# Spectral filter stage: groups 2 to 13 by pairs, with a second step of 64 x 64 matmuls, and the weights' bounds summed in PSUM

## The chip, the core and the metric

The kernel runs on one core of a Trainium2 chip. The core's engines each work through an instruction queue of their own: TensorE (PE, matmuls; its weight loads are shown as PEld), VectorE (DVE), ScalarE (ACT), GpSimd (POOL) and SyncE (SP), which here issues the DMA transfers. PE writes its sums to PSUM; the others read them there and write to SBUF, the on-chip memory from which PE reads. The metric is the device time of one execution in microseconds (us); lower is better. One execution of the kernel before was also recorded by the hardware profiler, and the profile's lines come from it.

## What is computed

Four residual layers over x of shape (2048, 640): a spectral filter A and a token-mixing MLP B, each applied twice, A, B, A, B. Cut to what matters:

```python
def A(x):                       # x already normalised over its last axis
    X = rfft2(x)                # 2048 x 321 complex
    return irfft2(X * (w_r + 1j * w_i))

def B(h):                       # h: normalised x
    u = gelu(einsum("sd,sf->df", h, w1) + b1)      # f = 1728
    return (einsum("df,fs->ds", u, w2) + b2).T

x = x + A(layernorm(x)); x = x + B(layernorm(x))
x = x + A(layernorm(x)); x = x + B(layernorm(x))
```

## The kernel before

Everything large is done by PE in float16, with each operand split into a high part and a low part (names ending in h and l); `mm3` (line 256) issues the three products high-high, high-low and low-high. The 2048 rows are split as 128 x 16, so a transform over them is two steps: one over 128 (S1), one over 16 (second step), with a factor between. The stages of one half of the kernel are:

1. **S1.** `run` (first layer) or the second part of `b1st` with `a0_tail` (second layer) normalises rows, folds them by symmetry (`a0_fold1`, `a0_fold2`) and multiplies by the tables tM. ACT writes the high part (`a0_s1h`) and DVE the low part (`a0_s1l`) of S1 to the tiles s1h and s1l.
2. **The filter, `a1` (lines 408 to 672).** It runs over 16 groups of 128 rows of the spectrum. For one group g, in order: `dstage` (D, the transform over the 640 columns by the table tD, 16 matmuls; its last columns come from stacked rests stk, loaded by DMA); `psplit` (ph on ACT, pl on DVE); `s2stage` (S, the second step of the transform by the table tS2: 12 matmuls of 128 x 128 with 321 columns); `product` (ta and tb on DVE, their difference and sum on POOL: the complex product with w); `xsplit` (xh on ACT, xl on DVE, with the scale sx) and `twice` (copies of 63 columns on ACT and POOL); `is2stage` (I, the inverse of the second step by tI2: 36 matmuls of 64 input rows, two halves q); `yevict` and `y2evict` on ACT and `y2split` on POOL, which write Y and the two parts of Y2. In the loop over g (line 584) PE runs D of g+1, I of g-3, S of g. The first group's S has a table of its own; the last group's S, product and split are done by thirds (`s2mm`, `last_product`).
3. **The way back, `a2`.** `id_mm` and `is1_mm` return to rows, the residual is added and the next normalisation is done.
4. **The MLP.** `b1st` (first layer): 14 products with w1 and 16 with w2. `b2nd` (last layer) does it in blocks. The weights come by `wload`, are scaled and split by `wsplit` (wh on ACT, wl on DVE). The scale of each weight tile is a power of two from a bound: `scan1` sums its squares on ACT, `total` adds over columns (DVE) and rows (one matmul with ones), `pow2` turns it into the scale on DVE. `scale_x` does the same for the filter's w, `scale_b` for b1, and the first `b1st` does one `scale1` for each weight tile. The last layer uses the scales again.

**Order.** Inside `a1`, `a2` and some other stretches `self.pin` is true: each engine then runs its instructions in the order in which the code issues them. Elsewhere the compiler may move them. [...]

**PSUM.** `big` (line 89) gives buffers of two banks, four of them in turn: a fifth request waits until the readers of the first are done. Buffers of the other tiles (`self.t` with a count) work in the same way: w has three, ta three, tb two, yt two.

Of the kernel before, what the change touches and what calls it, by code (L numbers as in the profile page):

```python
# [33 lines left out]
YS = 2.0 ** -14  # L34
I32 = mybir.dt.int32
# [21 lines left out]
class Layers:  # L57
    def __init__(self, nc, tc, A):
        self.nc, self.tc, self.A = nc, tc, A
        self.open = {}  # L60
# [38 lines left out]
    def setup(self):  # L99
        nc, A = self.nc, self.A  # L100
        base = self.base = self.push("base", side="left")
        self.psum = self.push("ps", bufs=4, space=PSUM)
# [81 lines left out]
    def scan(self, raw, out):  # L184

        n = raw.shape[1]
        self.T.activation(self.junk[:, :n], raw, AF.Square, accum_out=out)

    def scan1(self, m, cs=(0, 1)):
        if m < NFT + NJ:  # L190
            if 0 in cs:
                self.ssq = self.t(self.base, [128, 1, 2], F32, "sq", 2)
            for c in cs:
                self.scan(self.wraws[m][c], self.ssq[:, 0, c:c + 1])

    def scale1(self, m, at=None):
# [4 lines left out]
        for ps in self.total(self.ssq, at):  # L201
# [13 lines left out]
    def scale_x(self, pool):  # L215

        V, mm = self.V, self.PE.matmul
        ps = self.big()
        mm(ps[:NG, 0, :128], self.xq, self.eye, start=True, stop=True)
        m = pool.tile([NG, 1], F32, name="xm")  # L220
        V.tensor_reduce(m, ps[:NG, 0, :128], op=ALU.max, axis=mybir.AxisListType.X)
# [3 lines left out]
        mm(ps[:, 1, :NG], b, self.eye[:NG, :NG], start=True, stop=True)  # L225
        yield
        q = pool.tile([128, NG], F32, name="xqq")
        V.tensor_scalar(q, ps[:, 1, :NG], SMALL, XS ** -2, op0=ALU.max, op1=ALU.mult)
# [5 lines left out]
    def scale_b(self):  # L234

        b = self.base
        sq = b.tile([128, 1, 1], F32, name="sqs")
        bsq = b.tile([128, NFT], F32, name="bsq")
        self.T.activation(bsq, self.b1, AF.Square, accum_out=sq[:, 0])
        yield  # L240
        for ps in self.total(sq):
# [1412 lines left out]
```

## Time and profile before

| | us |
|---|---|
| median of 3 runs (1040.97 to 1043.22) | 1041.69 |
| profiled execution, its own time | 1044.98 |
| its span, first to last instruction | 1043.2 |
| S1 of the first layer | 0 to 57 |
| filter, first layer | 57 to 137 |
| way back, first layer | 137 to 197 |
| `b1st` and S1 of the second layer | 197 to 573 |
| filter, second layer | 573 to 647 |
| way back, second layer | 647 to 700 |
| `b2nd` | 700 to 1043 |

A line of the page or of a grouped view names an operation by engine, operation, what it writes and what it reads (buffer numbers left out), shape (partitions x elements) and type; behind x stands how often it ran, then its total busy time and the mean in ns of one, then how long its engine had been idle before it and what ended that. A timeline line begins with its start and its duration in us. Nearly all operations are recorded under line 49, a helper, so they are told apart by the names of their tiles: ps is a PSUM buffer, tD belongs to D, tS to S, tI to I.

### The profile page before, as it was taken

How to read it: one execution, taken by the hardware profiler on the slowest of the kernel's cores; microseconds unless marked ns; L12 is line 12 of the kernel's file. 1: busy time of each engine (PE TensorE's matmuls, PEld its weight loads, DVE VectorE, ACT ScalarE, POOL GpSimd, SP SyncE). 2: the span in 40 equal slices, each digit the busy share in tenths (PEclk: the TensorE clock that was granted, in tenths of full speed). 3: DMA queues.
4: the chain of work that ended last, by engine and by line, in shares of the span. 5: the costliest groups of instructions: out<-in, count | busy, mean ns of one | idle time of the engine just before them, and what ended most of it. 6: DMA issues, size and time to landing. Idle time of an engine off the chain costs nothing.

```text
span 1043.2 us, 20923 instructions
## 1 busy us (share of the span) xinstructions
PE 998.0 (96%) x8315; PEld 733.2 (70%) x8315; DVE 710.4 (68%) x1437; ACT 585.3 (56%) x910; POOL 273.3 (26%) x482
## 2 busy tenths in 40 slices
PE   4889989999999999999997998999999999999998
PEld 3768766677777777777775786666777777777776
DVE  7978947854333956666675796677655564987885
ACT  5857669765555555555542475894644454634532
POOL 6928867300000002221112586770000000000000
PEclk9999989999999999999998998999999999999999
DMA  7864336532222264444424543455422232445511
GB/s 225 312 198 133 100 114 193 197 105 81 82 81 77 71 221 142 139 134 122 122 79 148 158 129 99 150 179 184 132 87 84 72 107 88 139 145 176 165 44 51
DMA packets 55305, 137.38 MB, mean 132 GB/s; under 512 B 6540, under 2 KB 12328, under 8 KB 55208
## 3 DMA queue, kind: packets, MB, share of 16 engines
q1 hardware_dynamic: 55208, 136.06, 41.2%
q8 instruction: 65, 1.06, 0.4%
q14 instruction: 32, 0.26, 0.1%
HBM read 112.96 MB, written 23.07 MB: 130 GB/s over the span
## 4 chain that ended last, share of the span: by engine, by line
PE 66%; DVE 16%; ACT 6%; POOL 5%; DMA 4%; issue 3%; SPq 1%; POOLq 0%; ACTq 0%; DVEq 0%
PE ps L49 66%; DVE wl L49 3%; DVE f L49 3%; POOL eo L49 2%; DMA xt<-x 2%; DVE st L49 2%; DVE s1l L49 2%; ACT wh L49 1%; ACT z L49 1%; DVE hl L49 1%; ACT junk L49 1%; ACT xt L49 1%; DVE xt L49 1%; DMA raw<-w 1%; DVE ta L49 1%
## 5 line engine op out<-in xcount | busy, mean ns | idle before, releaser
L49 PEld LDWEIGHTS <-wh 128*128 128x128 f16 x2992 | 290.1, 98 | 113.9 <-issue 2.0
L49 PEld LDWEIGHTS <-wl 128*128 128x128 f16 x1616 | 157.9, 98 | 61.9 <-DVE wl L49 0.5
L49 PE MATMUL ps<-hh,wh 128*128 128x320 f16 x896 | 186.3, 299 | 0.8 <-ACT hh L49 0.8
L49 PE MATMUL ps<-hl,wh 128*128 128x320 f16 x896 | 184.7, 299 | 0.0
L49 PE MATMUL ps<-hh,wl 128*128 128x320 f16 x832 | 171.5, 299 | 0.2 <-DVE wl L49 0.2
L49 DVE SCALAR_TENSOR_TENSOR wl<-raw,s,wh 128x1024 f16<-128x1024 f32 (+2 forms) x88 | 103.6, 1181 | 87.6 <-ACT wh L49 86.7
L49 PE MATMUL ps<-uh,wl 128*128 128x320 f16 x448 | 133.1, 299 | 0.0
L49 PE MATMUL ps<-ul,wh 128*128 128x320 f16 x448 | 133.1, 299 | 0.0
L49 ACT ACTIVATE wh<-raw,s 128x1024 f16<-128x1024 f32 (+2 forms) x92 | 94.8, 1048 | 68.0 <-PE ps L49 62.1
L49 PE MATMUL ps<-uh,wh 128*128 128x320 f16 x416 | 124.3, 299 | 0.0
L49 ACT ACTIVATE junk<-raw 128x896 bf16<-128x896 f32 (+1 forms) x60 | 59.6, 994 | 47.8 <-DMA raw<-w 47.8
L49 POOL TENSOR_TENSOR r<-v,mh 128x1 f32<-128x1 f32 x64 | 35.7, 559 | 141.3 <-DVE nm L49 129.0
L49 DVE TENSOR_TENSOR xt<-xt,ps 128x320 f32<-128x320 f32 (+1 forms) x96 | 44.9, 490 | 39.9 <-ACT ec L49 25.8
L49 PE MATMUL ps<-u,wo 128*128 128x320 f16 x504 | 69.9, 299 | 0.0
L49 DVE TENSOR_TENSOR f<-eo 128x256 f32<-128x256 f32 (+1 forms) x128 | 40.0, 365 | 41.9 <-POOL eo L49 41.3
L49 PEld LDWEIGHTS <-wo 128*128 128x128 f16 x504 | 49.3, 98 | 19.1
L49 ACT ACTIVATE z<-xt,nb,r 128x640 f32<-128x640 f32 x31 | 28.5, 919 | 55.8 <-POOL z L49 43.7
L49 DVE BATCH_NORM_STATS2 st<-xt 128x6 f32<-128x320 f32 x128 | 56.2, 481 | 5.0 <-DMA xt<-x 4.8
L49 PE MATMUL ps<-ph,tS 128*128 128x321 f16 (+2 forms) x288 | 59.1, 290 | 0.0
L49 POOL TENSOR_TENSOR eo<-z 128x320 f32<-128x320 f32 x63 | 54.2, 880 | 17.0 <-ACT z L49 15.1
L49 PE MATMUL ps<-tM,f 128*128 128x128 f32 x160 | 39.1, 420 | 19.4 <-DVE f L49 19.4
L49 PE MATMUL ps<-tDi,yh 128*128 128x322 f16 x256 | 55.9, 309 | 1.6 <-ACT yh L49 1.6
(166 smaller groups left out, 1907.5 us busy)
## 6 DMA issues: line engine op xcount, KB each, us to landing
raw<-w SPq DMA_DIRECT2D x56, 512.0 KB
xt<-x SPq DMA_DIRECT2D x80, 320.0 KB
w<-w SPq DMA_DIRECT2D x48, 321.0 KB
x<-xt SPq DMA_DIRECT2D x48, 320.0 KB
raw<-w SPq DMA_DIRECT2D x32, 448.0 KB
raw<-w2z SPq DMA_DIRECT2D x32, 448.0 KB
out<-xt SPq DMA_DIRECT2D x15, 320.0 KB
stk<-rest SPq DMA_DIRECT2D x42, 64.0 KB
```

The source lines that it names most:

```text
L49: i = f(*a, **k)
```

## The change

- **Pairs.** Groups 2 to 13 are taken by pairs (a, b). S1 is stored so that the 64 rows which belong to two of a group's four row sets stand together. The table of the second step then consists of two blocks of 64 x 64 with zeros beside them, and only the blocks are multiplied: `s2pair` issues 48 matmuls of 64 x 64 with 321 columns, four (e, r) for each part and factor. Those with r = 0 write one PSUM buffer, those with r = 1 another; each buffer then holds one half of either group, so the filter's w, the rows of Y and the scale sx are put in that order too (`PG`, `lanes`, `k_rows`, gsel). Groups 0, 1, 14 and 15 keep 128 x 128 matmuls.
- **Order.** One iteration of the loop now issues D of a, I, D of b, I, and one S for both. The buffers of PSUM are three of the tag big and one of the tag one: in the filter every request names its tag, and only the second buffer of `s2pair` takes the single one; elsewhere every fourth request takes it.
- **Work moved between engines.** The scale sx moves from `xsplit` to the products (`times`), so xh is a copy and xl a subtraction; for even groups half of that subtraction is on POOL. The high part of Y2 is written by ACT from PSUM and no longer by POOL. w has four buffers, each loaded again right behind its product.
- **Bounds.** The sums of squares are written as bf16, one for each half of a tile. `total` has no reduction on DVE and adds the halves by one matmul each in PSUM, in spare columns of a buffer that is in use anyway. In `b1st` the bounds follow the end of a product instead of standing within the next.
- **Weights of the MLP.** The four quarters of wl of the first tile move from `a1` to `a2`, those of wh within `a1`; scan and wh of the second tile come some iterations later in `a2`.

The diff, cut to its core; the loop that it removes is in the code above.

```diff
+PG = 2, 14
...
-    def big(self):
+    def big(self, one=None):
+        if one is None:
+            self.turn += 1
+            one = self.turn % 4 == 0
+        tag, bufs = ("one", 1) if one else ("big", 3)
         self.n += 1
-        return self.psum.tile([128, 2, 512], F32, tag="big", name=f"ps{self.n}")
+        return self.psum.tile([128, 2, 512], F32, tag=tag, name=f"ps{self.n}", bufs=bufs)
...
     def total(self, sq, at=None):
 
+        ps = at() if at else self.big()[:, 0, :1]
         n = sq.shape[1]
-        b = self.t(self.base, [128, n], BF16, f"sqb{n}", 2 if n == 1 else 1)
-        with self.nc.allow_low_precision("a bound, with room to spare"):
-            self.V.tensor_reduce(b, sq, op=ALU.add, axis=mybir.AxisListType.X)
-        yield
-        ps = at() if at else self.big()[:, 0, :n]
-        self.PE.matmul(ps, self.ones, b, start=True, stop=True)
+        for i in range(n):
+            self.PE.matmul(ps, self.ones, sq[:, i:i + 1], start=i == 0, stop=i == n - 1)
         yield ps
...
-        self.s1h = p.tile([128, 80, 16, 8], F16, name=f"s1h{self.n}")
-        self.s1l = p.tile([128, 80, 16, 8], F16, name=f"s1l{self.n}")
+        self.s1h = p.tile([128, 80, 2, 16, 4], F16, name=f"s1h{self.n}")
+        self.s1l = p.tile([128, 80, 2, 16, 4], F16, name=f"s1l{self.n}")
...
-    def a0_s1h(self, j, pv, zs=ZS):
-        self.T.activation(self.s1h[:, :, j], pv, AF.Copy, scale=S1S / (zs * TS))
-    def a0_s1l(self, j, pv, zs=ZS):
-        self.V.scalar_tensor_tensor(
-            self.s1l[:, :, j], pv, S1S / (zs * TS), self.s1h[:, :, j], op0=ALU.mult, op1=ALU.subtract
-        )
+    def a0_s1h(self, j, pv, sc=S1S / (ZS * TS), q=slice(0, 80)):
+        pv = pv.rearrange("p a (b c) -> p a b c", c=4)
+        self.T.activation(self.s1h[:, q, :, j], pv, AF.Copy, scale=sc)
+    def a0_s1l(self, j, pv, sc=S1S / (ZS * TS), q=slice(0, 80)):
+        pv = pv.rearrange("p a (b c) -> p a b c", c=4)
+        h, l = self.s1h[:, q, :, j], self.s1l[:, q, :, j]
+        if sc == 1.0:
+            self.V.tensor_tensor(l, pv, h, op=ALU.subtract)
+            return
+        for b in range(2):
+            self.V.scalar_tensor_tensor(
+                l[:, :, b], pv[:, :, b], sc, h[:, :, b], op0=ALU.mult, op1=ALU.subtract
+            )
...
-        yv = self.Y.rearrange("p a b j (g q c) -> p g q (a b j) c", q=2, c=4)
-        y2 = [y.rearrange("p b j (g q c) -> p g q (b j) c", q=2, c=4) for y in self.Y2]
+        def lanes(y, g):
+            if PG[0] <= g < PG[1]:
+                y = y.rearrange("p b j (u e q c) -> p u q e (b j) c", e=2, q=2, c=4)
+                return y[:, g // 2, g % 2]
+            return y.rearrange("p b j (g q c) -> p g q (b j) c", q=2, c=4)[:, g]
...
         def y2evict(g, ps):
+            y2hi(g, ps)
...
             return yt
 
         def y2split(g, yt):
-            G.tensor_copy(y2[0][:, g], yt)
-            G.tensor_tensor(y2[1][:, g], yt, y2[0][:, g], op=ALU.subtract)
+            G.tensor_tensor(lanes(self.Y2[1], g), yt, lanes(self.Y2[0], g), op=ALU.subtract)
...
+            w = self.t(p, [128, 2, NL], F32, "w", 4)
...
+            ps = self.big(False)
...
+        sc = PQS / (S1S * TS)
+        def phi(ps):
             ph = self.t(p, [128, 2, 322], F16, "ph", 2)
             pl = self.t(p, [128, 2, 322], F16, "pl", 2)
...
             T.activation(ph[:, :, :NL], ps[:, :, :NL], AF.Copy, scale=sc)
...
+            return ps, ph, pl
+        def plo(ps, ph, pl):
             V.scalar_tensor_tensor(pl[:, :, :NL], ps[:, :, :NL], sc, ph[:, :, :NL], op0=ALU.mult, op1=ALU.subtract)
...
+            return ph, pl
+        def xhi(g, c, x):
+            T.activation(xs[g % 3][0][:, :, c], x, AF.Copy)
+        def xlo(g, c, x, r=slice(0, 2), e=V):
+            xh, xl = (q[:, r, c] for q in xs[g % 3])
+            e.tensor_tensor(xl, x[:, r], xh, op=ALU.subtract)
 
         def xsplit(g, c, x):
...
+            xhi(g, c, x)
+            xlo(g, c, x)
 
         def twice(g):
 
...
+        def s2pair(x):
+            ps = self.big(False), self.big(True)
+            for a, b in ((0, 0), (1, 0), (0, 1)):
+                for ri in range(2):
+                    for q in range(2):
+                        for e in range(2):
+                            for r in range(2):
+                                m = slice(64 * r, 64 * r + 64)
+                                mm(
+                                    ps[r][64 * e:64 * e + 64, ri, :NL], self.tS2[m, a, 0, 2 * ri + q, m],
+                                    x[e][b][m, q, :NL], start=a == b == q == 0, stop=b == q == 1,
+                                )
+            return ps
         def s2stage(g, ph, pl):
             sp = 1 if g == 0 else 0
-            ps = self.big()
+            ps = self.big(False)
             for ri in range(2):
                 for q in range(2):
                     a = tuple(self.tS2[:, h, sp, 2 * ri + q] for h in range(2))
-                    b = (ph[:, q, :NL], pl[:, q, :NL])
+                    b = tuple(x[q][:, :NL] if g == 0 else x[:, q, :NL] for x in (ph, pl))
                     self.mm3(ps[:, ri, :NL], a, b, q == 0, q == 1)
...
+        def times(o, ps, g, w, c=slice(0, NL)):
+            n = c.stop - c.start
+            V.scalar_tensor_tensor(
+                o, ps[:, :, c], self.sx[:, g:g + 1], w[:, c].unsqueeze(1).to_broadcast([128, 2, n]),
+                op0=ALU.mult, op1=ALU.mult,
+            )
+        def product(g, ps):
             ta, tb = (self.t(p, [128, 2, NL], F32, a, n) for a, n in (("ta", 3), ("tb", 2)))
...
+            times(ta, ps, g, w[g][:, 0])
+            times(tb, ps, g, w[g][:, 1])
             G.tensor_tensor(ta[:, 0], ta[:, 0], tb[:, 1], op=ALU.subtract)
...
+            gi = G.tensor_tensor(ta[:, 1], tb[:, 0], ta[:, 1], op=ALU.add)
+            if g + 4 < NG:
+                w[g + 4] = wload(g + 4)
+            return ta, gi
...
+        w = {g: wload(g) for g in range(4)}
+        ps2, pv, yt, ta = {}, {}, {}, {}
+        whole = slice(0, NL)
+        def phalves(ps):
+            x = tuple([self.t(p, [128, 322], F16, f"{a}{q}", 1) for q in range(2)] for a in ("ph", "pl"))
+            for q in range(2):
+                a, b, c = ps[:, q, :NL], x[0][q][:, :NL], x[1][q][:, :NL]
+                T.activation(b, a, AF.Copy, scale=sc)
+                V.scalar_tensor_tensor(c, a, sc, b, op0=ALU.mult, op1=ALU.subtract)
+            return x
+        def xbegin(g):
+            xh, _ = xs[g % 3]
+            xhi(g, whole, ta[g])
+            T.activation(xh[:, :, NL:], xh[:, :, 257:320], AF.Copy)
+        def xfinish(g):
+            x, (_, xl) = ta.pop(g), xs[g % 3]
+            if g % 2:
+                xlo(g, whole, x)
+            else:
+                xlo(g, whole, x, slice(1, 2), G)
+                xlo(g, whole, x, slice(0, 1))
+            G.tensor_copy(xl[:, :, NL:], xl[:, :, 257:320])
+        def evict(g):
+            yevict(g, pv[g])
+            yt[g] = y2evict(g, pv.pop(g))
+        d = dstage(0)
+        pa = phalves(d)
+        pb = phi(dstage(1))
+        ps2[0] = s2stage(0, *pa)
+        stack(4)
+        if first:
+            for _ in self.scale_x(p, d):
+                pass
+        pb = plo(*pb)
+        last = NG // 2 - 1
+        at = lambda c: lambda: old[:, 1, c:c + 1]
+        for i in range(1, NG // 2):
+            a, b, k = 2 * i, 2 * i + 1, 2 * i - 4
+            pa = phi(dstage(a))
+            if i == 1:
+                ta[0], _ = product(0, ps2.pop(0))
+                ps2[1] = s2stage(1, *pb)
+                pa = plo(*pa)
+                xbegin(0)
+                pb = phi(dstage(b))
+                ta[1], gi = product(1, ps2.pop(1))
+                pb = plo(*pb)
+            else:
+                pv[k] = old = is2stage(k)
+                evict(k)
+                x = product(a - 2, ps2.pop(a - 2))
+                if first and i in (3, 4):
+                    small = sb if i == 3 else self.scale1(0, at(401))
+                xfinish(k + 1)
+                ta[a - 2], _ = x
+                y2split(k, yt.pop(k))
+                d = dstage(b)
+                pb = phi(d)
+                for q in {5: (0,), 6: (1, 2), 7: (3,)}.get(i, ()):
+                    self.wsplit(0, self.quarter(q)[0], lo=False, part=self.quarter(q)[1])
+                pa = plo(*pa)
+                xbegin(a - 2)
+                if first and i in (3, 4):
+                    next(small)
+                pv[k + 1] = is2stage(k + 1)
+                ta[a - 1], gi = product(a - 1, ps2.pop(a - 1))
+                if first and i in (3, 4):
+                    next(small)
+                pb = plo(*pb)
+            stack(2 * i + 4)
+            if i < last:
+                ps2[a], ps2[b] = s2pair((pa, pb))
+            else:
+                ps2[a] = s2stage(a, *pa)
+            if i == 2:
+                nc.sync.dma_start(self.tDi, A["tDi"])
+            if i in (3, 4):
+                c = slice((i - 3) * 8, (i - 3) * 8 + 8)
+                nc.sync.dma_start(self.tIM[:, c], A["tIM"][:, c])
+            xfinish(a - 2)
             if k >= 0:
...
+                evict(k + 1)
+                y2split(k + 1, yt.pop(k + 1))
+            if i < last:
+                xbegin(a - 1)
+            if i == 1:
                 self.wload(0)
                 self.wopen(0)
...
+            if first and i in (2, 3):
+                if i == 2:
+                    sb = self.scale_b(at(400))
+                    next(sb)
+                self.scan1(0, (i - 2,))
 
...
+            if 3 < i < 8:
+                self.wsplit(0, self.quarter(i - 4)[0], hi=False, part=self.quarter(i - 4)[1])
             if first:
-                if i in (6, 7):
-                    self.scan1(1, (i - 6,))
-                if i == 8:
+                if i in (9, 10):
+                    self.scan1(1, (i - 9,))
+                if i == 11:
                     sc = self.scale1(1, at=lambda: ps1[:, 1, 400:401])
-                    next(sc)
-                if i == 10:
+                if i == 13:
                     next(sc)
             if i == 3:
                 self.wopen(1)
-            if i in (12, 13):
-                self.wsplit(1, (i - 12,), lo=False)
+            if i in (14, 15):
+                self.wsplit(1, (i - 14,), lo=False)
...
+        def scales(ps, *ms):
+            for q, m in enumerate(ms):
+                if m < NFT + NJ:
+                    for _ in self.scale1(m, lambda: ps[:, 1, 400 + q:401 + q]):
+                        pass
...
                     if ft == NFT - 1 and 6 <= j:
                         usplit(j - 6, uf[j - 6])
+            scales(ps, *{0: (2,), 1: (3,), 2: (4, 5)}.get(ft, (ft + 3,)))
...
+            scales(ps, m + 3)
...
-            r_in = j16 * 8 + c8
+            r_in = c8 // 4 * 64 + j16 * 4 + c8 % 4
...
+    a = slice(*PG)
+    out[a] = out[a].reshape(-1, 2, 2, 64).transpose(0, 2, 1, 3).reshape(-1, 128).copy()
...
-    t["tM32"] = (m1 * TS).astype(np.float32)
+    t["tM32"] = (m1 * S1S).astype(np.float32)
```

More of the change, by code (lines that the diff above doesn't have):

```diff
@@ L186, in scan @@
         n = raw.shape[1]
-        self.T.activation(self.junk[:, :n], raw, AF.Square, accum_out=out)
+        junk = self.junk[:, :n] if len(raw.shape) == 3 else self.junk[:, 0, :n]
+        with self.nc.allow_low_precision("a bound, with room to spare"):
+            self.T.activation(junk, raw, AF.Square, accum_out=out)
     def scan1(self, m, cs=(0, 1)):
@@ L396, in a0_tail @@
             q = slice(t0 * 16, t1 * 16)
-            T.activation(self.s1h[:, q, j], pv, AF.Copy, scale=sc)
-            V.scalar_tensor_tensor(
-                self.s1l[:, q, j], pv, sc, self.s1h[:, q, j], op0=ALU.mult, op1=ALU.subtract
-            )
+            self.a0_s1h(j, pv, q=q)
+            self.a0_s1l(j, pv, q=q)
     def s1_all(self, j, fh, fl):
@@ L438, in y2hi @@
         def y2hi(g, ps):
-            T.activation(y2[0][:, g], pairs(ps, 256, 384), AF.Copy, scale=YS)
+            T.activation(lanes(self.Y2[0], g), pairs(ps, 256, 384), AF.Copy, scale=YS)
         def y2lo(g, ps):
@@ L481, in dstage @@
         def dstage(g):
-            ps = self.big()
-            part = lambda t: tuple(s[:, t * 16 + g].rearrange("p a b -> p (a b)") for s in (self.s1h, self.s1l))
+            ps = self.big(False)
+            part = lambda t: tuple(s[:, t * 16 + g].rearrange("p q a b -> p (q a b)") for s in (self.s1h, self.s1l))
             for c, bk, o0, o1, k in CL:
@@ L749, in a2 @@
                 ps1 = is1_mm(eo.pop(i - 1), i - 1)
-            if first and i == 10:
+            if first and i == 13:
                 next(sc)
```

177 lines of the change are left out of this document (43 added, 134 removed).

## The prediction

> **What bounds the kernel now.** I read the page's span and engines first: PE is busy 96% of it. Then, by windows, the filter stage, which runs twice, and the matrix stage behind the first of them (391 to 553).
>
> ```profile
> span 1043.2 us, 20923 instructions
> PE 998.0 (96%) x8315; PEld 733.2 (70%) x8315; DVE 710.4 (68%) x1437; ACT 585.3 (56%) x910; POOL 273.3 (26%) x482
> 391.00:553.00 162.00, 162.00 (x1319) 119.79 (x1318) 102.60 (x288) 86.55 (x126) 36.17 (x84) 1.00 0.40 124
> 80.00:88.00 8.00, 8.00 (x130) 6.58 (x128) 7.04 (x10) 6.22 (x14) 6.66 (x10) 1.00 0.52 151
> 112.00:120.00 8.00, 8.00 (x127) 6.27 (x125) 8.00 (x11) 5.59 (x11) 7.34 (x11) 1.00 0.50 146
> ```
>
> A windows row gives the stretch, then busy time of PE, PEld, DVE, ACT, POOL, the granted clock, DMA share and GB/s. PE is never idle in 80 to 88, but DVE has 7.0 and POOL 6.7 of 8 us: matmuls that go save time only until the next queue is full. In 112 to 120 DVE is full as well. The timeline shows what a group costs there:
>
> ```profile
> 81.12 0.31 PE L49 MATMUL ps<-ph,tS 128*128 128x321 f16 x1
> 82.64 0.30 PE L49 MATMUL ps<-ph,tS 128*128 128x321 f16 x1
> 82.78 0.30 PE L49 MATMUL ps<-tD,s1h 128*128 128x160 f16 x2
> 83.85 0.23 PE L49 MATMUL ps<-tD,stk 96*128 96x161 f16 x1
> 84.02 0.28 PE L49 MATMUL ps<-tI,xh 64*128 64x128 f16 x4
> 84.98 0.22 PE L49 MATMUL ps<-tI,xl 64*128 64x128 f16 x2
> 85.13 0.31 PE L49 MATMUL ps<-ph,tS 128*128 128x321 f16 x1
> 82.98 0.83 DVE L49 TENSOR_TENSOR ta<-ps,w 128x642 f32<-128x642 f32 x1 [0.16 <-PE ps L49]
> 83.72 0.82 DVE L49 TENSOR_TENSOR tb<-ps,w 128x642 f32<-128x642 f32 x1
> 84.86 0.83 DVE L49 SCALAR_TENSOR_TENSOR pl<-ps,ph 128x642 f16<-128x642 f32 x1 [0.32 <-ACT ph L49]
> 85.61 1.16 DVE L49 SCALAR_TENSOR_TENSOR xl<-ta,sx,xh 128x642 f16<-128x642 f32 x1
> ```
>
> The second step S (12 matmuls) runs 81.12 to 82.78, 1.66 us, (82.64 - 81.12)/11 = 0.138 each. The column transform D (16) runs to 84.02, 1.24 us, of which about 0.10 is empty at the end: its last matmul starts at 83.85, and 160 columns take (83.85 - 82.78)/15 = 0.071. The inverse I (36 of 64 rows) takes 1.11 us, again with about 0.1 empty at its end. Together 4.01 us a group. I's matmuls come every (84.98 - 84.02)/34 = 0.028 us although each streams 128 columns, which at D's rate would be 0.057: two row halves of the array work at once.
>
> **The pairs on PE.** For groups 2 to 13, 2 x 12 full matmuls become 48 of 64 x 64: twelve quartets, in each the four quarters of the array. If a quartet takes one 0.138 slot, S for two groups takes 1.66 instead of 3.32. PE needs per pair 2 x 1.24 + 2 x 1.11 + 1.66 + 0.1 (one more change of the array's shape, now between S and D) = 6.46 us, against 8.02. The other bound, from rows: only what I shows, two at a time, gives 24 x 0.138 = 3.32; nothing at all overlapped, 6.6, and I's 0.028 speaks against that. I take 1.66: I's 36 pairs of load and matmul show neither an issue limit (0.028 x 4 = 0.11 a quartet) nor a cost of loading.
>
> [...]
>
> **The pairs on the other queues.** What waits is DVE: its order in an iteration is ta and tb of group a-2, xl of a-3, pl of a, ta and tb of a-1, pl of b, half of xl of a-2. PE's S writes two buffers, of which the second comes from the new one-buffer tag. It is still held by group a-1 until that group's tb. So each S waits for six DVE operations, the first of which waits for the last S. Behind S on PE stand D and I of the next pair, and all of DVE's next products wait for it: a delay here is paid in full. Durations:
>
> ```profile
> L49 DVE SCALAR_TENSOR_TENSOR xt<-ps,c,xt 128x640 f32<-128x640 f32 x16 | 14.1, 882 | 5.0 <-ACT xt L49 5.0
> L49 DVE TENSOR_TENSOR hl<-hf,hh 128x640 f16<-128x640 f32 x32 | 23.8, 817 | 0.0
> 122.57 0.88 DVE L49 SCALAR_TENSOR_TENSOR xl<-ta,sx,xh 128x642 f16<-128x642 f32 x1
> L49 ACT ACTIVATE ph<-ps 128x642 f16<-128x642 f32 x30 | 21.2, 707 | 42.1 <-PE ps L49 42.1
> L49 ACT ACTIVATE hh<-hf 128x640 f16<-128x640 f32 x32 | 22.6, 730 | 0.5
> L49 ACT ACTIVATE xh<-xh 128x126 f16<-128x126 f16 x32 | 9.9, 308 | 1.0
> L49 ACT ACTIVATE Y<-ps 128x512 f32<-128x512 f32 x30 | 17.4, 581 | 3.1 <-PE ps L49 3.1
> L49 ACT ACTIVATE Y2h<-ps 128x256 f16<-128x256 f32 x4 | 1.5, 380 | 1.3 <-PE ps L49 1.3
> L49 ACT ACTIVATE yt<-ps 128x256 f32<-128x256 f32 x28 | 10.5, 375 | 1.1 <-POOL Y2l L49 1.1
> L49 POOL TENSOR_TENSOR ta<-tb,ta 128x321 f32<-128x321 f32 x30 | 28.1, 936 | 0.0
> L49 POOL TENSOR_TENSOR ta<-ta,tb 128x321 f32<-128x321 f32 x30 | 23.7, 791 | 46.8 <-DVE tb L49 46.8
> L49 POOL TENSOR_TENSOR Y2l<-yt,Y2h 128x256 f16<-128x256 f32 x28 | 20.9, 746 | 2.2
> L49 POOL COPY xl<-xl 128x126 f16<-128x126 f16 x32 | 9.7, 303 | 1.5 <-DVE xl L49 1.5
> ```
>
> Consecutive DVE operations overlap by 0.08 (tb starts 0.74 after ta). The products carry the scale now, so they are priced as the 0.882 row: 0.80 each. The low part of x becomes a plain subtraction: 0.82 alone as hl, but xl took 1.16 at 85.61, beside POOL, and 0.88 at 122.57, so with that factor 1.3 it is 1.08. pl is 0.75. Chain: 2 x 0.80 + 1.08 + 0.75 + 2 x 0.80 = 5.03; from the end of S to ta 0.20 (82.78 to 82.98), back to PE 0.05, S 1.66: **6.94, taken as a period of 7.0 us**. PE then idles about half a microsecond a pair.
>
> The rest fits under 7.0. ACT per pair: 2 x (0.71 + 0.73 + 0.31 + 0.58 + 0.38 + 0.38) = 6.2 (the high part of Y2 is new there). POOL: 2 x (0.94 + 0.79 + 0.75 + 0.30) = 5.6 and about 0.85 for its half of xl, between the 0.791 and 0.936 rows: 6.4. The three-buffer ring: the second I takes the buffer of D of a, free when pl of a is done 3.4 us into the period, and I is due at 3.5; all others have over 0.5 us. SP's new order, w behind each product and the stack behind the second, still issues a stack more than a period before its D. In the first layer the products now need the scale sx, whose small operations stand ahead of them on DVE in both kernels. In iterations 5 to 7 ACT also splits four quarters of weights, 0.72 each as before; 6.2 + 1.44 exceeds 7.0 once, 0.7 in all.
>
> **Where the stage ends.** I compare the start of S of group 14, behind which the order is as before.
>
> ```profile
> 73.05 1.54 PEld L49 LDWEIGHTS <-tS 128*128 128x128 f16 x12
> 122.13 3.40 PEld L49 LDWEIGHTS <-tS 128*128 128x128 f16 x48
> 583.37 1.54 PEld L49 LDWEIGHTS <-tS 128*128 128x128 f16 x12
> 632.07 3.40 PEld L49 LDWEIGHTS <-tS 128*128 128x128 f16 x48
> ```
>
> At 73.05 S of group 2 starts. Now it must also have ph of group 3, whose D ends just then: 0.85 later (0.14 and 0.71), so the first pair ends at 73.05 + 0.85 + 1.66 = 75.6. Five periods of 7.0, the 0.7 of ACT and the last two D and I (4.7) give 116.0 against 122.13: 6.1 saved. In the second layer 583.37 gives 626.3 against 632.07: 5.8. Of this the full DVE of 112 to 120 is a part: its weight quarters move to the stage behind.
>
> **The other edits.** The new layout of S1 is written in runs of 4 elements. Y2h is, too, and its 0.380 for 256 elements stands beside 0.375 of yt, written in one run: no price. Outside the filter every fourth allocation takes the single buffer, so the depth stays four.
>
> ```profile
> 248.44 0.17 PE L49 MATMUL ps<-sqb,ones 128*128 128x1 bf16 x1
> 248.46 0.43 PE L49 MATMUL ps<-hh,wh 128*128 128x320 f16 x2
> 136.50:197.00 60.50, 59.55 (x355) 39.72 (x355) 39.61 (x138) 50.55 (x81) 41.49 (x62) 0.97 0.53 167
> L49 DVE SCALAR_TENSOR_TENSOR wl<-raw,s,wh 128x512 f16<-128x512 f32 x8 | 6.2, 772 | 0.0
> L49 DVE SCALAR_TENSOR_TENSOR pl<-ps,ph 128x321 f16<-128x321 f32 x4 | 2.0, 495 | 5.9 <-ACT ph L49 5.9
> ```
>
> Bounds: 31 one-column matmuls become 61; one costs PE about 0.025 (248.44 to 248.46). In the matrix stage PE is full, so 30 x 0.025 = 0.8 lost; the 31 reductions on DVE save nothing there (102.6 of 162 busy). They now stand at the end of a product, 3 us behind their scans, so PE should not wait; if it does, up to 1 us for each of about 28. In the first layer six small operations enter DVE's chain in iteration 4: 0.6 lost. Four quarters of wl (0.77) move into the stage of the window 136.5 to 197, where DVE has 21 us free; without that cover 3 us a layer. s1l becomes two of 0.495 instead of one of 0.82, hidden but for the end of the matrix stage: 0.3 lost. At the tail, cheaper x parts gain 0.3 a layer.
>
> Sum: 6.1 + 5.8 + 0.6 - 0.8 - 0.6 - 0.3 = 10.8 us. The profiled execution took 1045.0 (span 1043.2 and 1.8 around it), so 1034.2 on its own account; it lies 3.3 over the median, 1041.7, which becomes **1030.9 us**. There are ten periods, so the time is 1030.9 + 10 x (P - 7.0).
>
> **Rivals.**
> *Loading binds the quartets.* Four loads of 64 columns must fit into 0.138. The only slower form of load in the trace, float32, gives a ceiling:
>
> ```profile
> 56.89 1.63 PE L49 MATMUL ps<-tM,f 128*128 128x128 f32 x10 [0.24 <-DVE f L49]
> ```
>
> 0.163 for 128 columns, waits included, so at most 0.08 for 64. One after another 0.33 a quartet (S 3.9, P 9.2, 1053); two at once 0.16 (S 1.96, P 7.3, 1034). The middle, 0.245: S 2.94, P 8.2, 1043. For it: no quarter-array load is in the trace. Against: I's loads of 64 rows are hidden in 0.028.
>
> [...]
>
> *Slower: only row halves overlap.* Two matmuls of a quartet read the same 64 rows for different output columns; the trace shows no two such at once. S stays 3.32, and with the wait for tb in front P = 5.28 + 3.32 = 8.6: 1047. It decides from S = 2.8 (P 8.08), where the 10.8 are gone. The change then doesn't do what it says.
>
> *Longer queue:* DVE's operations stretch beside POOL as xl did, or I waits for pl: P 7.5, 1036. *Shorter:* DVE hides, PE's 6.46 binds: P 6.5, 1026.
>
> **Numbers.** Forecast (1028 to 1034) 50%; longer queue 13%; shorter 8%; loading 18%, of which 4 faster, 5 the same, 9 slower; row halves 11%. Faster by over 0.2%, about what a measurement of this kernel tells from none, 75%; same 5%; slower 20%. 1023.5 to 1042.5 holds the first three and half of the loading case, 80%.
>
> **What would show it.** Right: 48 matmuls of 64 x 64 in about 1.7 us, periods near 7.0, PE waiting for DVE tb about 0.5 a pair, DVE over 85% busy there. Wrong: quartets over 0.2 us; PE waiting for ACT, POOL or a stack instead; any wait of PE for a scan in the matrix stage; or PE waiting in the stage behind the filter.

## The result, and the profile after

The changed kernel takes **1034.66 us** in the median of 4 runs (1033.62 to 1036.68) beside 1042.45 before on the same chip: ratio 0.9929, 95% interval 0.9908 to 0.9949. The profiled execution is the slowest of the four, 1036.7 with a span of 1034.9. The changed kernel, unaltered, was run once more with the experiments: 1034.75 (1033.38 to 1035.07) beside 1044.64 before, ratio 0.9899 (0.9883 to 0.9916). Its profile is called "again" below.

The page of the changed kernel, its span and engines:

```profile
span 1034.9 us, 21565 instructions
PE 982.0 (95%) x8633; PEld 723.4 (70%) x8633; DVE 695.4 (67%) x1423; ACT 592.8 (57%) x938; POOL 267.1 (26%) x468
```

Windows of two pairs of the second filter, columns as in the prediction:

```profile
595.79:602.46 6.67, 6.67 (x157) 5.87 (x154) 5.93 (x9) 5.59 (x13) 6.36 (x10) 1.00 0.49 130
602.46:609.12 6.66, 6.66 (x156) 5.85 (x152) 5.91 (x9) 5.58 (x13) 6.34 (x10) 1.00 0.49 135
```

PE has 16 us less to do, of which the span shows 8.3. A pair takes 6.66 us, not 7.0, and PE looks busy throughout. The timeline, the second step of one pair on PE, then the order of DVE and two operations of POOL in the pair before it:

```profile
602.46 1.47 PE L50 MATMUL ps<-ph,tS 64*64 64x321 f16 x32
603.63 0.84 PE L50 MATMUL ps<-pl,tS 64*64 64x321 f16 x16
604.41 0.32 PE L50 MATMUL ps<-tD,s1h 128*128 128x160 f16 x2
597.84 0.89 DVE L50 SCALAR_TENSOR_TENSOR ta<-ps,sx,w 128x642 f32<-128x642 f32 x1 [0.74 <-PE ps L50]
598.64 0.88 DVE L50 SCALAR_TENSOR_TENSOR tb<-ps,sx,w 128x642 f32<-128x642 f32 x1
599.44 0.82 DVE L50 TENSOR_TENSOR xl<-ta,xh 128x642 f16<-128x642 f32 x1
600.17 0.82 DVE L50 SCALAR_TENSOR_TENSOR pl<-ps,ph 128x642 f16<-128x642 f32 x1
600.91 0.88 DVE L50 SCALAR_TENSOR_TENSOR ta<-ps,sx,w 128x642 f32<-128x642 f32 x1
601.70 0.88 DVE L50 SCALAR_TENSOR_TENSOR tb<-ps,sx,w 128x642 f32<-128x642 f32 x1
598.78 0.73 POOL L50 TENSOR_TENSOR Y2l<-yt,Y2h 128x256 f16<-128x256 f32 x1
599.60 1.27 POOL L50 TENSOR_TENSOR ta<-ta,tb 128x321 f32<-128x321 f32 x1
```

Finer windows of the second step alone show what the busy share hides. They hold PE and PEld only, and the number in brackets behind PE's busy time counts the matmuls in flight:

```profile
602.45:602.50 0.05, 0.04 (x1) 0.04 (x2) 1.00 0.01 0
602.50:602.60 0.10, 0.10 (x1) 0.06 (x2) 1.00 0.01 0
602.60:602.65 0.05, 0.05 (x5) 0.02 (x4) 1.00 0.26 82
602.65:602.75 0.10, 0.10 (x5) 0.10 (x7) 1.00 0.43 133
...
602.80:602.90 0.10, 0.10 (x8) 0.10 (x4) 1.00 0.65 185
602.90:602.95 0.05, 0.05 (x12) 0.05 (x7) 1.00 0.49 144
```

One matmul starts at 602.46, into the buffer that is free. The next, which writes the single buffer, does not start until tb has ended at 601.70 + 0.88 = 602.58; then four start at once, and four more every 0.15 or less. PE does wait for tb, about 0.15 us a pair, under a matmul that counts as busy. The loop closes: 12 quartets of 0.138 after 602.61 end at 604.27, and D follows at 604.41. In the pair before, S began at 595.79, so from the quartets' start to ta it is 597.84 - 595.79 - 0.15 = 1.90, from ta to the end of the second tb 4.74, from there to the next quartets 0.03: 6.67.

Where the time went, in us. The stretches are cut at the starts of the second step S, of the inverse transform behind the tail, of the products of each matrix, and at the ends of the spans:

| Stretch | before | changed | again |
|---|---|---|---|
| first filter, S of group 0 to S of group 14 | 58.7 | 51.8 | 52.2 |
| its tail, to the first inverse transform | 14.3 | 13.8 | 14.5 |
| stage behind it | 55.6 | 55.4 | 55.9 |
| first matrix stage, w1 | 179.5 | 181.0 | 181.0 |
| the same, w2, to S of group 0 | 205.0 | 206.5 | 206.1 |
| second filter, S of group 0 to S of group 14 | 55.6 | 50.2 | 47.9 |
| its tail | 14.3 | 14.5 | 14.5 |
| stage behind it | 53.9 | 54.9 | 54.8 |
| last matrix stage, to the end of the span | 342.9 | 343.1 | 343.1 |

So the filters give 12.3 us in the first profile and 14.2 in the second, and about 4 of it are given back, most of it in the first matrix stage and in the stage behind the second filter.

### The profile page after: what moved, and what is told of

It is laid out like the page before. It is cut to its first block, busy times and chain, and to the rows that moved or that the text cites. A ratio compares the mean times of both kernels' runs of the same rounds, so it can differ in the third digit from the quotient of the medians.

```text
span 1034.9 us, 21565 instructions
## 1 busy us (share of the span) xinstructions
PE 982.0 (95%) x8633; PEld 723.4 (70%) x8633; DVE 695.4 (67%) x1423; ACT 592.8 (57%) x938; POOL 267.1 (26%) x468
## 4 chain that ended last, share of the span: by engine, by line
PE 67%; DVE 12%; ACT 7%; DMA 6%; POOL 4%; issue 3%; SPq 0%; ACTq 0%; POOLq 0%; DVEq 0%
PE ps L50 67%; DMA raw<-w 3%; DVE f L50 3%; POOL eo L50 3%; DVE wl L50 2%; DMA xt<-x 2%; DVE s1l L50 2%; DVE st L50 1%; ACT junk L50 1%; ACT z L50 1%; ACT fh L50 1%; DVE fl L50 1%; ACT wh L50 1%; DVE xt L50 1%; DMA stk<-rest 1%
## 5 line engine op out<-in xcount | busy, mean ns | idle before, releaser
L50 PEld LDWEIGHTS <-wh 128*128 128x128 f16 x2992 | 290.2, 98 | 116.0 <-issue 3.8
L50 PEld LDWEIGHTS ps<-tM,f 128*128 128x128 f32 x160 | 32.0, 288 | 26.6 <-DVE f L50 26.1
```

What stands on the lines that cost most here:

```text
L50: i = f(*a, **k)
```

## The experiments

**e1_full_s: the second step in full matmuls, all else kept.**

```diff
-PG = 2, 14
+PG = 2, 2
...
-            for a, b in ((0, 0), (1, 0), (0, 1)):
+            for e in range(2):
                 for ri in range(2):
                     for q in range(2):
...
+                        c = tuple(self.tS2[:, h, 0, 2 * ri + q] for h in range(2))
+                        self.mm3(ps[e][:, ri, :NL], c, tuple(y[:, q, :NL] for y in x[e]), q == 0, q == 1)
```

> The pairs' order, buffers and all else as in the changed kernel; only the second step is again two times 12 full matmuls, with rows in the old order. If the quartets are the gain: S of a pair takes 24 x 0.138 = 3.3 us instead of 1.95, the period goes from 6.66 to about 8.0, and twelve pairs cost 12 x 1.35 = 16 us: 1051 us (1048 to 1053), slower than before the change. Rival: DVE's chain or the pairs' order sets the period and the quartets only part of it: under 1045.

Measured: 1046.37 us, ratio 1.0017 (1.0004 to 1.0031). The period is 8.01, as expected: S starts every 8.01 us in the second layer (585.13 to 633.22 for six pairs). The time is 12 over that of the second run of the changed kernel and not 16, under the 1048 that was the least expected: the small waits of the first pairs vanish under the longer S. In the first layer the wait for ph goes from 1.73 to 0.33, and in the second the way from S of group 0 to the first pair's S takes 6.4 instead of 7.3. The quartets are the gain; pairs without them are no faster than the kernel before.

**e6_rows_only and e8_cols_only: the order of the 48 matmuls.**

```diff
-            for a, b in ((0, 0), (1, 0), (0, 1)):
-                for ri in range(2):
-                    for q in range(2):
-                        for e in range(2):
+            for e in range(2):
+                for a, b in ((0, 0), (1, 0), (0, 1)):
+                    for ri in range(2):
+                        for q in range(2):
                             for r in range(2):
```

In e8 it is r that goes outermost, and e innermost.

> The same 48 quarter matmuls of a pair in another order: the two groups one after the other, so that matmuls that follow each other alternate the row half and its buffer, and not the column half. If a quartet is short because all four quarters work at once: now two at a time, 24 x 0.146 = 3.5 instead of 1.76, the period 8.3 and the time 1034.7 + 12 x 1.7 = 1055. Rival: matmuls of this form simply come every 0.037 whatever stands beside them: 1034.7.

> The 48 quarter matmuls of a pair in a third order: first all that read the upper rows, then all that read the lower rows, so that matmuls that follow each other alternate the column half and read the same 64 rows. If column halves work at once as row halves do: 0.073 a matmul except at the seam, where both run, S about 3.1, the period about 7.8 and the time near 1047, as with row halves alone. Rival: two column halves don't overlap (the price at which the change would have lost): 0.14 a matmul, S over 5.5, period over 10, 1075 or more.

Measured: 1047.45 and 1049.32 us, one run each. The timeline of a pair's S in e6:

```profile
601.81 1.43 PE L50 MATMUL ps<-ph,tS 64*64 64x321 f16 x16
602.98 0.40 PE L50 MATMUL ps<-pl,tS 64*64 64x321 f16 x2
603.09 0.33 PE L50 MATMUL ps<-ph,tS 64*64 64x321 f16 x2
603.12 0.43 PE L50 MATMUL ps<-pl,tS 64*64 64x321 f16 x3
...
603.53 0.85 PE L50 MATMUL ps<-ph,tS 64*64 64x321 f16 x10
604.22 0.71 PE L50 MATMUL ps<-pl,tS 64*64 64x321 f16 x8
604.86 0.32 PE L50 MATMUL ps<-tD,s1h 128*128 128x160 f16 x2
```

Sixteen matmuls take 1.17 us, 0.073 each, half of the 0.138 of a full matmul: two at a time. In e8 it is (605.77 - 604.64)/16 = 0.071:

```profile
604.64 1.29 PE L50 MATMUL ps<-ph,tS 64*64 64x321 f16 x16
605.77 0.30 PE L50 MATMUL ps<-pl,tS 64*64 64x321 f16 x2
```

So row halves overlap, column halves overlap, and only the mixed order has four at once. S is 3.05 and 2.91, the periods 7.77 and 7.62. The 8.3 and 1055 expected of e6 missed the seam: where one half's last eight (pl) and the other's first matmuls (ph) stand in the queue together, they run side by side.

**e7_short_low: half the columns in 32 of the 48 matmuls.**

```diff
             for a, b in ((0, 0), (1, 0), (0, 1)):
+                n = 160 if a or b else NL
...
-                                    ps[r][64 * e:64 * e + 64, ri, :NL], self.tS2[m, a, 0, 2 * ri + q, m],
+                                    ps[r][64 * e:64 * e + 64, ri, :n], self.tS2[m, a, 0, 2 * ri + q, m],
```

> Leaves out columns 160 to 320 of the 32 low-part matmuls of a pair; loads and their number stay. If the length of the streamed columns sets a quartet: S falls from 1.76 by 16 x 0.037 = 0.59; both PE's 6.66 and DVE's chain contain S, so the period falls to POOL's 6.36 to 6.4 and the time by ten times 0.27 or so, 1032. Rival: loading 64 columns four times sets the 0.146: S and the period stay, 1034.7, and the 0.138 of a full matmul is only by chance near it.

Measured: 1034.69 us in one run, period 6.59. That looks like the rival, but finer windows of S (columns as in those above), and the timeline, tell another story:

```profile
599.95:600.05 0.10, 0.08 (x1) 0.08 (x2) 1.00 0.61 179
600.05:600.35 0.30, 0.24 (x1) 0.03 (x2) 1.00 0.17 48
600.35:600.40 0.05, 0.00 (x0) 0.00 (x0) 1.00 0.00 0
600.40:600.45 0.05, 0.04 (x4) 0.03 (x6) 1.00 0.00 0
```

```profile
601.64 0.32 PE L50 MATMUL ps<-tD,s1h 128*128 128x160 f16 x2
599.49 0.87 DVE L50 SCALAR_TENSOR_TENSOR tb<-ps,sx,w 128x642 f32<-128x642 f32 x1
603.34 1.29 DVE L50 TENSOR_TENSOR xl<-ta,xh 128x642 f16<-128x642 f32 x1
603.22 0.73 POOL L50 TENSOR_TENSOR Y2l<-yt,Y2h 128x256 f16<-128x256 f32 x1
```

After the first matmul at 599.97 PE waits for tb (599.49 + 0.87 = 600.36), 0.43 instead of 0.15. From 600.40 to D at 601.64 is 1.24, against 602.61 to 604.41, 1.80, with full columns: 0.56 shorter, the 0.59 expected. Four full quartets and 0.14 to D leave 1.24 - 0.55 - 0.14 = 0.55 for eight of 160 columns, 0.07 each: loading four times 64 columns fits into 0.07, and streaming alone sets 0.138. The time does not follow, because DVE's xl now starts while POOL's Y2l runs and takes 1.29. In the changed kernel it started as Y2l ended (599.44), took 0.82, and POOL's next operation (599.60, 1.27) was the one stretched, off the chain. The chain behind the single buffer takes back what S gave.

**e9_longer_chain: one more DVE operation between two products.**

```diff
+        def extra(x):
+            V.tensor_copy(self.t(p, [128, 321], F16, "extra", 1), x[0][:, 0])
...
+                extra(x)
                 pa = plo(*pa)
                 xbegin(a - 2)
```

> One more DVE operation a pair, a copy of 128 x 321 that nobody reads, between the products of one group and pl of the next, that is in the chain from the end of S to the tb that frees the single buffer. In the changed kernel that chain takes 4.62 + 2.05 with S, 6.67, beside PE's 6.66. If the chain has no slack, the period rises by the copy's length (0.3 to 0.5), the time by ten times that, 1038 to 1040, and PE waits for DVE tb. Rival: PE alone sets the period and DVE's 0.74 of idleness a pair takes the copy: 1034.7 within 0.5.

Measured: 1050.18 us in one run, period 8.17. The copy had to wait for POOL's sum besides, so it lengthened the chain by far more than its 0.8:

```profile
606.84 0.82 DVE L50 TENSOR_TENSOR xl<-ta,xh 128x642 f16<-128x642 f32 x1
608.30 0.86 DVE L50 CAST extra<-ta 128x321 f16<-128x321 f32 x1 [0.64 <-POOL ta L50]
609.08 0.81 DVE L50 SCALAR_TENSOR_TENSOR pl<-ps,ph 128x642 f16<-128x642 f32 x1
609.95 0.29 PE L50 MATMUL ps<-tI,xh 64*128 64x128 f16 x4 [1.13 <-DVE pl L50]
611.53 0.74 PE L50 MATMUL ps<-ph,tS 64*64 64x321 f16 x16 [0.15 <-DVE tb L50]
```

The longest wait that the profile shows is not the expected one for tb but I's 1.13 for pl, the last reader of the buffer that I takes. It doesn't set the period: one matmul of S starts at 611.06 behind I, and the rest still waits for tb, which ends at 610.61 + 0.87 = 611.48.

Without the copy pl starts 0.73 after xl (599.44 to 600.17 above); here 2.24 after: 1.51 more, and the period grew from 6.66 to 8.17, by 1.51. The chain has no slack at all; DVE's 0.74 of idleness a pair, ahead of ta, helps nothing, since it is spent waiting for S. Ten such periods are the 15 us between the two times.

**e2_old_sums: the bounds of the matrix stages as before.** The functions `step` and `total` of the kernel before for the matrices from the third on, and its reduction on DVE.

```diff
+                if i in (6, 7):
+                    step(m + 2)
...
+                if i == 26 and m + 3 < NFT + NJ:
+                    step(m + 3)
...
-            scales(ps, m + 3)
```

> The changed kernel with the bounds of the matrix stages as before the change: a reduction on DVE, one matmul a bound, in a buffer of its own in the middle of a product. If the sums at the end of each product (and PE's waits for scans behind them) are what these stages lost: from the first product of the first matrix stage to the first S of the second filter 387.4 becomes about 385, the wait of PE for ACT's junk (0.4) is gone, and the time is 1034.7 - 2 = 1032.7. Rival: the loss lies elsewhere (clock, first products, waits for hh): within 0.7 of 1034.7.

Measured: 1037.06 us, ratio 0.9924 (0.9906 to 0.9942). The wait for junk is gone, but the sums, which again take buffers of their own, now wait for these:

```profile
230.82 0.16 PE L50 MATMUL ps<-sqb,ones 128*128 128x1 bf16 x1 [1.24 <-ACT q L50]
419.86 0.16 PE L50 MATMUL ps<-sqb,ones 128*128 128x1 bf16 x1 [3.42 <-DVE xt L50]
```

The two stretches take 390.4 us, 3 more than the 387.5 of the changed kernel and not 2 less; the two waits are 4.7 of it. Behind the second, PE also runs 3.4 us at half clock (420.6 to 424.0), by an estimate 1.7 more. The run does not isolate the price of the new sums, which stays open.

**e3_w3 and e4_ph_first: the start of the filter.**

```diff
-            w = self.t(p, [128, 2, NL], F32, "w", 4)
+            w = self.t(p, [128, 2, NL], F32, "w", 3)
...
-        w = {g: wload(g) for g in range(4)}
+        w = {g: wload(g) for g in range(3)}
```

```diff
-                xbegin(0)
                 pb = phi(dstage(b))
+                xbegin(0)
```

> The filter's weights w in three buffers instead of four, each loaded one group later, as before the change. If the fourth load in flight delays the stack at the second filter's start: PE's wait for the stack there falls from 2.02 to about 1.2, the clock stays whole in S of group 1 as it did before the change (2.8 us at half clock, so 1.4 less): 1034.7 - 2.2 = 1032.5. Rival: the stack's own issue and length set that wait, and w comes late instead: 1034.7 within 0.6, with new waits of DVE for w.

> One swap on ACT in the first pair of each layer: the high part of D of group 3 ahead of the high part and doubling of x of group 0 (1.05 us). If PE's waits for ph (1.72 in the first layer, 0.54 in the second) come from that order: they shrink by up to 1.05 and 0.5, and the time is 1033.2. Rival: the product of group 1 on DVE, or x of group 0, is late next and takes it all: within 0.5 of 1034.7.

Measured: e3 1034.46, ratio 0.9900 (0.9884 to 0.9917); e4 1031.38, ratio 0.9877 (0.9857 to 0.9898). The rows show PE's wait for the stack at the second filter's start and, behind it, a window with the clock (third number from the right). They are, in order, the wait in the first profile, wait and window in the profile called again, the wait in e3, and the window in the first profile. The wait in again is put down to no releaser (issue):

```profile
576.33 0.23 PE L50 MATMUL ps<-tD,stk 96*128 96x160 f16 x1 [2.02 <-DMA stk<-rest]
```

```profile
576.44 0.23 PE L50 MATMUL ps<-tD,stk 96*128 96x160 f16 x1 [1.40 <-issue]
576.50:580.30 3.80, 3.80 (x43) 3.19 (x44) 1.96 (x4) 1.67 (x3) 1.46 (x2) 1.00 0.80 220
```

```profile
578.07 0.23 PE L50 MATMUL ps<-tD,stk 96*128 96x160 f16 x1 [1.45 <-DMA stk<-rest]
```

```profile
576.50:580.30 3.80, 3.80 (x24) 2.68 (x22) 0.83 (x1) 1.64 (x3) 0.92 (x2) 0.55 0.72 211
```

With four buffers the wait was 1.40 and the clock whole, with three 1.45: the fourth buffer is not the cause, and the 2.3 us that the second filter's start lost in the first profile (50.2 against 47.9) belong to that execution. The same was expected of the second run before it ran: 7.4 us from S of group 0 to the first pair's S instead of 9.6, and it took 7.3. The swap of e4 does what it should in the first layer only:

```profile
74.13 1.16 PE L50 MATMUL ps<-ph,tS 64*64 64x321 f16 x28 [1.72 <-ACT ph L50]
```

```profile
73.54 1.16 PE L50 MATMUL ps<-ph,tS 64*64 64x321 f16 x28 [0.54 <-ACT ph L50]
```

From S of group 1 to here it is 4.93 in the changed kernel and 3.74 in e4 (started at 69.20 and 69.80): 1.2 gained. In the second layer the wait is 0.54 in both, with nothing gained. Its median is the lowest of all versions that were run, but the profile accounts for only 1.2 of the 3.4 us between it and the changed kernel's second run, the two ratios' intervals overlap, and e10 below, with the same swap, takes 1033.61. So the rest of the 3.4 is not shown to come from the swap.

**e5_tail_one: a fourth buffer at the tail.**

```diff
-        def is2stage(g):
-            ps = self.big(False)
+        def is2stage(g, one=False):
+            ps = self.big(one)
...
-        pv[k - 2] = is2stage(k - 2)
+        pv[k - 2] = is2stage(k - 2, True)
```

> The inverse of group 12 at the tail takes the single buffer, so the tail has four buffers in turn as it had before the change, instead of three. If PE's waits there (ACT yt 1.26, ACT Y 1.31 or 0.8) are waits for a buffer: the first goes, the last inverse starts about 1.3 earlier, ACT's last evictions bind, and each tail is 0.8 shorter: 1034.7 - 1.6 = 1033.1. Rival: the doubled low part of x on POOL is late next and takes it all: within 0.4.

Measured: 1033.73, ratio 0.9894 (0.9879 to 0.9908). One wait takes the place of the other; the row of the changed kernel and that of e5:

```profile
123.45 0.29 PE L50 MATMUL ps<-tI,xh 64*128 64x128 f16 x4 [1.26 <-ACT yt L50]
```

```profile
124.17 0.29 PE L50 MATMUL ps<-tI,xl 64*128 64x128 f16 x2 [1.16 <-DVE xl L50]
```

The tails take 14.47 and 14.46, as again (14.47 and 14.48). The rival holds for the tails, with DVE and not POOL: the low part of x is late next. The median is 1.0 under that of again, more than the rival's 0.4, but nothing of it lies in the tails, and the intervals overlap.

**e10_start and e11_start_a2: moving small work.** e10 has e4's swap and writes the sums beside the second D; e11 also has the scan and scale of the second weights back at the old iterations.

```diff
-        at = lambda c: lambda: old[:, 1, c:c + 1]
+        at = lambda c: lambda: d[:, 1, c:c + 1]
```

```diff
-                if i in (9, 10):
-                    self.scan1(1, (i - 9,))
-                if i == 11:
+                if i in (6, 7):
+                    self.scan1(1, (i - 6,))
+                if i == 8:
...
-            if i in (14, 15):
-                self.wsplit(1, (i - 14,), lo=False)
+            if i in (12, 13):
+                self.wsplit(1, (i - 12,), lo=False)
```

> The swap on ACT in the first pair (ph ahead of x), and the two small sums of the third and fourth pair of the first layer written beside the second D instead of into the first inverse's buffer, so that they need not wait for ACT yt (0.46). If those waits are paid in full: first pair 1.2 shorter in the first layer as in the run with the swap alone, the third and fourth periods 7.54 and 7.0 together 0.7 shorter: 1034.7 - 1.9 = 1032.8. Rival: the small operations on DVE hold the chain anyway and only the swap's 1.2 shows: 1033.5.

> As the run before, and in the stage behind the first filter the scan, scale and high part of the second weights back at the iterations they had before the change (6 to 13 instead of 9 to 15). If PE's later waits for ACT's hh at the first product (0.53 and 0.26 against 0.26 and 0.16) come from that shift: the first product is 0.4 shorter, in the first and possibly the second layer: 0.4 to 0.8 under the run before. Rival: ACT is late there with other work, no difference.

Measured: e10 1033.61, ratio 0.9888 (0.9871 to 0.9904). The sum waits longer than before (0.46 for ACT yt in the changed kernel):

```profile
86.62 0.16 PE L50 MATMUL ps<-sqs,ones 128*128 128x1 bf16 x1 [1.06 <-ACT ph L50]
```

The third and fourth periods are 7.87 and 7.48, longer than 7.54 and 7.0, and the next is 6.49 instead of 7.06: together 0.2 longer. Only the swap shows. e11: 1045.86, ratio 1.0009 (0.9994 to 1.0023). The stage behind the first filter takes 67.5 us instead of 55.9, since PE waits 8.4 us in it for ACT's e and then runs 6.8 us at half clock (170.9 to 177.7). The changed kernel has no such wait, and whole clock there:

```profile
159.57 1.06 ACT L50 ACTIVATE junk<-raw 128x1024 bf16<-128x1024 f32 x1 [3.75 <-DMA raw<-w]
169.70 1.06 ACT L50 ACTIVATE junk<-raw 128x1024 bf16<-128x1024 f32 x1 [5.88 <-DMA raw<-w]
171.59 2.52 PE L50 MATMUL ps<-e,tIM 128*128 128x322 f32 x4 [5.64 <-ACT e L50]
```

The second weights load into the buffers that the low quarters of the first, now split in this very stage, still read; the scan at its old place waits for that load, and ACT's eviction behind it, and PE behind that. The later place of the scans belongs to the move of the quarters. The first product's 0.4 did come back in part (waits for hh of 0.27 and 0.16 instead of 0.53 and 0.27), drowned in this.

## Why the prediction was right, and where it was off

- **S of a pair, 1.66.** Right. Four quarters start together, a quartet takes 0.138, and e1, e6 and e8 show what it would be without. The loading rival falls with e7 (four loads in 0.07), the row-halves rival with e6 and e8. The records of the loads last about 0.105 each, and 48 of them stand in the 1.69 from 602.46 on, so several run at a time. The 0.1 in PE's 6.46 for one more change of the array's shape was an estimate from the two gaps of about 0.1 around I; that the change of shape makes such a gap is not shown, but 0.14 lies between the quartets' end and D (604.27 to 604.41).
- **What bounds a pair: DVE's chain behind the single buffer.** Right in mechanism, mis-sized: "5.03 + .20 + .05 + 1.66 = 6.94, taken as 7.0" measured 6.66. The term that failed is xl "1.08", stretched beside POOL as before the change: in the new order it takes 0.73 from start to start, 0.35 less. That the order spares xl was not foreseen. e7 shows that the stretch itself is real: move the meeting point, and xl takes 1.29. The step "PE then idles about half a microsecond" is so 0.15, and the page of the profile does not call it idle. The "shorter" rival (PE binds) reads the same from the busy shares; e9 speaks against it, for a bound on PE alone would have swallowed part of the 1.51.
- **Start of S of group 14.** Forecast 116.0, measured 115.56: right by luck, since two errors cancel, a shorter period and first pairs lengthened by ACT's order (1.2), the small sums and the weight quarters (periods 7.54, 7.0 and 7.06). In the second layer "626.3" became 622.5; the two filters together saved 12.3 and 14.2 instead of 11.9.
- **The bounds: "0.8", and "PE should not wait".** Too small. The first matrix stage lost 2.6 to 3.0 us in all where 0.8 + 0.3 was forecast. In w1 the rows name about 1.2 of 1.5: 14 more sums of 0.028, 0.4 for junk, 0.4 for hh at the first product. The 0.4 for junk is a wait of PE for a scan in the matrix stage, which the prediction had named as a sign of being wrong. In w2 the fh wait at the end varies between runs from nothing to 1.9 (0.8 before, 1.2 after, none in again), and part of the loss is the clock: up to the first D of the second filter w2 takes 200.5 before, 201.7 after and 200.5 in again, and that D takes 4.45, 4.71 and 5.52, since it runs at half clock for its first 2.0, 2.5 and 4.2 us. How much of the rest is due to the sums is open (e2).
- **Tails, "0.3 gained" each.** Wrong: 0.1 lost in the second layer (14.34 to 14.48), between 0.1 lost and 0.5 gained in the first. The 0.5 is no gain of the change that is shown: in that one tail the clock stayed whole to its end (129.4), in the other five of the table it fell to half on the way. Three buffers instead of four put a wait of 1.26 there, which the prediction, costing the ring only inside the loop, did not see; e5 shows that its removal alone would not help.
- **The stages behind, nothing.** The first, within 0.4. The second lost 1.0, without any wait of PE: its beginning runs at half clock for longer, as the last section shows.

Together: 10.8 us forecast, 7.8 in the first comparison, 9.9 in the second. The time of 1034.66 lies 3.8 above the 1030.9 of the forecast and just outside its narrower range of 1028 to 1034. By the profiles' spans (8.3 and 9.9) the filters gave 1 to 3 more than forecast (11.9 less 0.6 for the small operations), and the rest of the kernel lost some 3.5 more.

## What to carry to other kernels

In this kernel, small matmuls that fill the four quarters of the array came four for the price of one (0.138 us), if neighbours in the queue differ in row half and column half; the gain then stops at the next queue, here a single PSUM buffer that six DVE operations must pass. A wait can hide under one matmul already started (0.15 us a pair here): count matmuls in flight in windows of 0.05 us rather than trust a full busy share. When a step that frees a buffer is moved, move with it every load and every in-order reader that stands behind that buffer; in e11 PE waited 8.4 us for want of that.

## What was not expected of the hardware

In these profiles the granted clock falls to half for 3.4 us or a multiple of it (3.4, 6.8, 10.2), behind stretches in which PE waits: in the 3.4 us ahead of the fall it was busy for 1.58 before (638.8 to 642.3) and for 1.44 after (628.0 to 631.4). Behind the second filter it was at half for 6.8 us before (642.3 to 649.1) and 10.2 after (631.4 to 641.6); from the first inverse transform on, 2.7 and 4.7 of that, and half of the difference is the 1.0 lost there. In again it is 4.5 us at half clock and 0.9 lost. A window inside each of the first two:

```profile
642.50:648.50 6.00, 3.73 (x32) 2.20 (x32) 1.64 (x6) 3.14 (x9) 3.46 (x11) 0.50 0.00 0
```

```profile
631.50:641.50 10.00, 7.46 (x62) 4.65 (x63) 2.56 (x9) 4.59 (x13) 3.41 (x11) 0.50 0.01 2
```

Whether such a piece follows a wait differs from run to run, as at the second filter's start (e3): the clock from 576.50 to 580.30 was 0.55 in the first profile, behind a wait of 2.02, and 1.00 in again, behind 1.40. One caution on reading the clock: the windows of the kernel before print 1.00 for its first 50 us, those of the changed kernel 0.50 for about 30 of them, but ten tM matmuls take 2.62 us there in both (at 31.50 and at 31.80), against 1.63 in the prediction's row at 56.89. So the first stage ran at half clock before the change too, and the difference in the printed clock does not come from the change.

Matmuls of different quarters did not all start in the order of the code: in e6 all pl of the first group stand in the code, which is pinned there, ahead of the second group's ph, and from 602.98 to 603.53 they start alternately. So the order in which the code issues, which the section on the kernel before gives for such stretches, does not hold for these starts. Nor do the rows show that all other engines read PSUM: only DVE (350 before, 367 after) and ACT (263 and 291) have rows that read ps. And of two operations of DVE and POOL on SBUF alone, the one that started while the other ran was stretched: xl from 0.82 to 1.29 behind Y2l in e7, POOL's addition to 1.27 behind xl in the changed kernel.
